# Reordering turns 3 to 14 of an attention backward kernel: K blocks, softmax, V quarters and stores in another order

## The chip, the cores and the metric

The kernel runs on one core of a Trainium2 chip. The metric is the device time of one execution in microseconds (us). Engines are named as in the profile: PE is TensorE, DVE is VectorE, ACT is ScalarE, POOL is GpSimd, SP is SyncE, which here issues almost all DMA transfers.

## The reference

One query per head attends to 8192 keys and values, for 32 heads of width 128, and the gradients of q, k and v are wanted as well as the output. All tensors are bfloat16.

```
B, H, Sq, Skv, Dh = 1, 32, 1, 8192, 128
def _fwd_reference(q, k, v):
    scale = q.shape[-1] ** -0.5
    scores = jnp.einsum('bhqd,bhkd->bhqk', q, k) * scale
    attn = _softmax(scores, axis=-1)
    return jnp.einsum('bhqk,bhkd->bhqd', attn, v)
...
_out, _vjp = jax.vjp(_f, q, k, v)
_grads = _vjp(grad_out)          # dq, dk, dv
```

With one query this is, per head: s = K q, p = softmax(s), out = pᵀV, dp = V·grad_out, ds = p (dp − Σ p dp) · scale, dq = dsᵀK, and the two large results dK = ds ⊗ q and dV = p ⊗ grad_out. K, V, dK and dV are 64 MiB each, 134 MB read and 134 MB written in all.

## The kernel before

**Tiling.** Two heads form one turn t; there are HP = 16 turns. In a turn K and V are tiles of 128 partitions x 128 rows x 128 columns, 4 MiB each. `k_in` has three such buffers, `v_in` two. dK and dV are written in place over K and V and stored from there, so a buffer's next load waits for its store.

**Steps of a turn** (NB = 8 blocks of 16 rows per partition):

- `k_block(t, c)`, lines 197 to 210: DVE transposes block c of K in 32x32 squares into an `XK` buffer (three buffers in pool `xkp`), and PE takes four matmuls from it into the scores bank `s`. A fourth transpose must wait until the first block's matmuls have left its buffer.
- `s_back`, `s_top`, `s_exp`, `s_sum`, `p_of`: the softmax. The scores come back by a DVE transpose, the maximum goes over PE and back to DVE (`nbias`), ACT takes the exponential, PE adds up (`s_sum`), DVE takes the reciprocal (`rinv`), ACT writes `p_rep` and the window `win_p`.
- dp = V·grad_out in two ways in the "wide" turns 3 to 14 (`wide(t)`): half of the rows by `v_part` = `v_bank` (PE transposes into one of three PSUM banks `psT`) + `v_copy` (ACT copies them out), followed by `v_scores` (PE); the other half by `v_block` (DVE transpose into an `XK` buffer) followed by `v_wide` (four PE matmuls). Both add into the bank `dp_ps`.
- `contract(t, "p")`: PE, 32 matmuls, out from V and `win_p`; `contract(t, "ds")`: PE, 32 matmuls, dq from K and `win_ds`.
- `outer(t, "p", r)` writes block r of dV, `outer(o, "ds", r)` writes block r of dK, both on DVE (line 366). The dK blocks of turn o = t − 1 are written in turn t by `dk(a, b)`, which stores dK after its last block.
- `v_back`, `pd_sum`, `ds_of`: dp comes back by a DVE transpose (line 315), Σ p dp goes over PE (line 324), `pdt` (line 329), ds on DVE, `win_ds` on ACT (line 244).
- `gather` takes out or dq of four turns out of the accumulator: out in turns 3, 7, 11 (behind `contract(t, "ds")`), dq in turns 4, 8, 12 (behind `pd_sum`). `prepare(t + 1)` spreads the next q and grad_out rows over the partitions.

**Order.** The instructions are put on each engine in the order of the program text (`manual_schedule`), and each engine works in that order. In a wide turn before the change DVE does: dK blocks 0 to 4; softmax with V blocks 0 and 1 between its steps and dK block 5; V blocks 2 and 3; dK blocks 6 and 7; dV blocks 0 and 1; `v_back`; dV block 2; `ds_of`; then dV blocks 3 to 7 alternating with K blocks 0 to 4 of the next turn; K blocks 5 to 7. SP issues per turn: store dK(t − 1), store dV(t), load K(t + 2), load V(t + 2).

Turns 1, 2 and 15 use another branch (all of V by `v_part`), turn 16 only finishes dK(15) and the small results.

Of the kernel before, what the change touches and what calls it, by code (L numbers as in the profile page):

```python
# [15 lines left out]
NB = 8  # L16
# [11 lines left out]
def kernel(  # L28
# [143 lines left out]
    dq_all = consts.tile([P, H], F32)  # L172

    def prepare(t):
        x = st[t] = {}
        x["m"] = psM.tile([P, 512], F32, tag="m", name="m_ps")
        for s in range(2):
            nc.tensor.matmul(x["m"][s * HF:(s + 1) * HF, 256:512],
                             lhsT=ident[0:H, 2 * t + s:2 * t + s + 1].to_broadcast([H, HF]),
                             rhs=rows[:].rearrange("h a d -> h (a d)"), start=True, stop=True, skip_group_check=True)  # L180
        x["qd"] = small.tile([P, 2, D], BF16, tag="qd", name="qd")
        nc.scalar.copy(x["qd"][:].rearrange("p a d -> p (a d)"), x["m"][:, 256:512])
# [12 lines left out]
            nc.scalar.copy(do_wide[a * QD:(a + 1) * QD, :, a * QD + SL - 1], do_four[a * QD:(a + 1) * QD, :, t])  # L195

    def k_block(t, c):
        x = st[t]
        X = xkpool.tile([P, BN, NW, QD], F32, tag="XK", name="XK_sb")
        nc.vector.transpose(X[:], Kt[t][:, c * BN:(c + 1) * BN, :].rearrange("p n d -> p (n d)").bitcast(F32).rearrange(  # L200
            "p (n w j) -> p n w j", n=BN, w=NW))
        if c == 0:
            x["s"] = psS.tile([P, 512], F32, tag="s", name="s_ps")
        cols = X[:].rearrange("p n w i -> p (n w i)").bitcast(BF16).rearrange(
            "p (n w i e) -> p w e n i", n=BN, w=NW, e=2)
        for w in range(NW):
            for e2 in range(2):
                nc.tensor.matmul(x["s"][:], lhsT=q_win[:, 2 * w + e2, SL - 1 - c:SL - 1 - c + P],  # L208
                                 rhs=cols[:, w, e2], start=(c == 0 and w == 0 and e2 == 0),
                                 stop=(c == NB - 1 and w == NW - 1 and e2 == 1), skip_group_check=True)  # L210
# [45 lines left out]
    def wide(t):  # L256
        return 3 <= t < HP - 1
# [22 lines left out]
    def v_scores(t, z):  # L280
        x = st[t]
        cols = x.pop(("XV", z)).rearrange("p m s -> p (m s)").bitcast(BF16).rearrange(
            "p (m s e) -> p e m s", s=P, e=2)
        if z == 0:
            x["dp"] = psD.tile([P, 512], F32, tag="dp", name="dp_ps")
        at = SL - 2 - 2 * z
        for e2 in range(2):
            for b in range(NQ):
                nc.tensor.matmul(x["dp"][b * QD:(b + 1) * QD, :], lhsT=do_win[:, b // 2, e2, at:at + QD],  # L289
                                 rhs=cols[:, e2, :, b * QD:(b + 1) * QD],  # L290
                                 start=(z == 0 and e2 == 0), stop=(not wide(t) and z == NZ - 1 and e2 == 1), skip_group_check=True)

    def v_block(t, r):

        X = xkpool.tile([P, NM, NW, QD], F32, tag="XK", name="XV_blk")
        nc.vector.transpose(X[:], Vt[t][:].rearrange("p n d -> p (n d)").bitcast(F32).rearrange(  # L296
            "p (m r w j) -> p m r w j", r=SL, w=NW, j=QD)[:, :, SL // 2 + r])
        st[t]["XW", r] = X

    def v_wide(t, r):  # L300
        cols = st[t].pop(("XW", r))[:].rearrange("p n w i -> p (n w i)").bitcast(BF16).rearrange(
            "p (n w i e) -> p w e n i", n=NM, w=NW, e=2)
        at = SL - 1 - (SL // 2 + r)
        for w in range(NW):
            for e2 in range(2):
                nc.tensor.matmul(st[t]["dp"][:], lhsT=do_wide[:, 2 * w + e2, at:at + P], rhs=cols[:, w, e2], start=False,  # L306
                                 stop=(r == SL // 2 - 1 and w == NW - 1 and e2 == 1), skip_group_check=True)

    def rows_in(x):
        return x.rearrange("p (m r) -> p m r", r=SL)  # L310
# [40 lines left out]
    def gather(t, which):  # L351
        S_ = backs.tile([P, 4, D], F32, tag="back", name="S_" + which)
        nc.scalar.copy(S_[:].rearrange("p j d -> p (j d)"), acc.pop(which)[:])
        bank, to = st[max(st)]["m"], (o_all if which == "p" else dq_all)
        pick = lane[:].rearrange("p (w j) -> p j w", j=4)
        at = 8 if which == "p" else 16
        for j in range(4):
            nc.tensor.matmul(bank[:, at:at + 2 * ST], lhsT=S_[:, j, :], rhs=pick[:, j, :],
                             start=(j == 0), stop=(j == 3), skip_group_check=True)
        nc.scalar.copy(to[:, 2 * (t - ST + 1):2 * (t + 1)], bank[:, at:at + 2 * ST])  # L360
# [104 lines left out]
    for t in range(1, HP + 1):  # L465
        o = t - 1
        now = t < HP
        parts = 4 if o == HP - 1 else 2 if o == HP - 2 else 1

        def dk(a, b):  # L470
            for r in range(a, b):
                outer(o, "ds", r)
                if (r + 1) % (NB // parts) == 0:
                    store(o, "ds", parts, r * parts // NB)

        blocks = now and wide(t)

        if blocks:

            dk(0, 5)  # L480
            s_back(t)
            s_top(t)
            for m in range(3):
                v_bank(t, m)
            v_block(t, 0)
            rs = s_exp(t)
            for m in range(3):
                v_copy(t, m)
            v_block(t, 1)
            v_part(t, 3)  # L490
            s_sum(t, rs)
            v_scores(t, 0)
            v_wide(t, 0)
            dk(5, 6)
            p_of(t)
            v_part(t, 4)
            v_part(t, 5)
            v_block(t, 2)
            v_wide(t, 1)
            v_part(t, 6)  # L500
            v_part(t, 7)
            v_block(t, 3)
            contract(t, "p")
            v_scores(t, 1)
            v_wide(t, 2)
            v_wide(t, 3)
            weights_do(t + 1)
            if wide(t + 1):
                weights_wide(t + 1)
        else:  # L510
            dk(0, 3)
            if now:
                v_part(t, 3)
                v_part(t, 4)
                s_back(t)
                s_top(t)
                v_scores(t, 0)
                v_part(t, 5)
                v_part(t, 6)
                rs = s_exp(t)  # L520
                for m in (7, 8, 9):
                    v_bank(t, m)
                s_sum(t, rs)
                v_copy(t, 7)
                v_copy(t, 8)
            dk(3, 4)
            if now:
                p_of(t)
                v_copy(t, 9)
                v_scores(t, 1)  # L530
                v_part(t, 10)
                v_part(t, 11)
                contract(t, "p")
                v_part(t, 12)
                v_part(t, 13)
                v_scores(t, 2)
                v_part(t, 14)
                v_part(t, 15)
                v_scores(t, 3)
                if t + 1 < HP:  # L540
                    weights_do(t + 1)
                    if wide(t + 1):
                        weights_wide(t + 1)
        if not now:
            dk(4, NB - 1)
            results()
            dk(NB - 1, NB)
            break
        dk(6 if blocks else 4, NB)
        fine = t == HP - 1  # L550
        outer(t, "p", 0)
        outer(t, "p", 1)
        if fine:
            store(t, "p", 4, 0)
        v_back(t)
        pd_sum(t)
        if t % ST == 0:
            gather(o, "ds")
        outer(t, "p", 2)
        ds_of(t)  # L560
        contract(t, "ds")
        if t % ST == ST - 1:
            gather(t, "p")
        if t + 1 < HP:
            prepare(t + 1)
        else:
            gather(t, "ds")
        for r in range(3, NB):
            outer(t, "p", r)
            if fine and r % 2:  # L570
                store(t, "p", 4, r // 2)
            if t + 1 < HP and t != 1 and r >= HALF - 1:
                k_block(t + 1, r - HALF + 1)
        if not fine:
            store(t, "p")
        if t == 1:
            for c in range(HALF + 1):
                k_block(t + 1, c)
        if t + 1 < HP:
            for c in range(HALF + 1, NB):  # L580
                k_block(t + 1, c)
                if not wide(t + 1):
                    v_part(t + 1, c - HALF - 1)
            if t + 2 < HP:
                weights_q(t + 2)
        if t + 2 < HP:
            load_k(t + 2)
            load_v(t + 2)
# [32 lines left out]
```

## Time and profile before

| quantity | before |
|---|---|
| median of 3 runs (lowest to highest) | 635.55 us (635.34 to 635.67) |
| the profiled execution's own time | 635.21 us |
| its span, first to last instruction | 633.4 us |
| granted PE clock, mean | 0.829 |
| DVE busy | 558.7 us (88%) |
| PE busy | 426.1 us (67%) |
| ACT busy | 156.9 us (25%) |
| bytes moved by DMA | 268.92 MB, mean 425 GB/s |

The span is 1.8 us shorter than the execution's own time, and that execution is 0.34 us below the median. Busy times are unions of an engine's instructions; a share of the whole span is an average over the start, sixteen turns and the end.

### The profile page before, as it was taken

The page shows a single profiled execution, that of the slowest core. Times are in us where ns is not written, and L with a number is a line of the kernel's source. Part 1 is how long each engine was busy: PE and PEld are TensorE (multiplying, and loading weights), DVE is VectorE, ACT ScalarE, POOL GpSimd, SP SyncE. Part 2 cuts the span into 40 slices and gives each one's busy share as a digit, 9 for nine tenths or more (in the row PEclk, how much of TensorE's full clock was granted, in tenths as well). Part 3 has the DMA queues.
Part 4 walks back from the last instruction along what each step waited for, and adds up shares of the span by engine and source line. Part 5 has one row for each costly group of instructions (what it writes and reads, how often), then busy time and mean ns, then how long its engine had stood idle before and what let it go on. Part 6 is the DMA issues. An engine that isn't in the chain of part 4 may idle for free.

```text
span 633.4 us, 7259 instructions
## 1 busy us (share of the span) xinstructions
PE 426.1 (67%) x2876; PEld 227.8 (36%) x2876; DVE 558.7 (88%) x662; ACT 156.9 (25%) x407; POOL 9.3 (1%) x27
## 2 busy tenths in 40 slices
PE   5968686478665767457776586756758667387950
PEld 2635252243423425134352342524415243152630
DVE  7688988989989899798998979899898998989891
ACT  1616052040311304114041220412304032040610
POOL 2000000000000000000000000000000000000000
PEclk9979597887788887878878888888898788987955
DMA  8999999999999999999999999999999999999996
GB/s 364 431 429 403 447 431 429 430 428 426 436 432 434 433 430 435 429 430 427 429 430 430 432 434 435 432 435 436 426 435 431 432 429 432 426 435 429 416 422 269
DMA packets 12177, 268.92 MB, mean 425 GB/s; under 512 B 1520, under 2 KB 1520, under 8 KB 1520
## 3 DMA queue, kind: packets, MB, share of 16 engines
q1 hardware_dynamic: 12048, 268.46, 98.9%
q8 instruction: 22, 0.36, 0.2%
q14 instruction: 11, 0.09, 0.0%
q10 hardware_dynamic: 96, 0.02, 0.0%
HBM read 134.23 MB, written 134.23 MB: 424 GB/s over the span
## 4 chain that ended last, share of the span: by engine, by line
DMA 42%; DVE 30%; PE 15%; issue 7%; ACT 3%; DVEq 0%; ACTq 0%; SPq 0%
DMA out_dram<-K 22%; DMA K<-in_k_dram 18%; DVE XK_sb L200 12%; DVE K L366 10%; PE T_ps L272 6%; DVE V L366 5%; PE dp_ps L306 3%; PE s_ps L208 2%; ACT XV_sb L278 2%; PE acc_p L344 2%; PE dp_ps L289 1%; DVE sT L215 1%; DMA rows<-in_grad_out_dram 1%; PE m_ps L223 1%; PE acc_ds L344 1%
## 5 line engine op out<-in xcount | busy, mean ns | idle before, releaser
L208 PE MATMUL s_ps<-XK_sb,q_win 128*128 128x512 bf16 x512 | 149.7, 433 | 50.0 <-DVE XK_sb L200 46.8
L200 DVE STREAM_TRANSPOSE XK_sb<-K 128x1024 f32<-128x1024 f32 x128 | 152.4, 1224 | 14.4 <-DMA K<-in_k_dram 12.0
L366 DVE TENSOR_TENSOR V<-p_rep,qd 128x2048 bf16<-128x2048 bf16 x128 | 151.9, 1205 | 2.9 <-ACT K L278 2.4
L366 DVE TENSOR_TENSOR K<-ds_rep,qd 128x2048 bf16<-128x2048 bf16 x128 | 147.8, 1209 | 0.1
L208 PEld LDWEIGHTS <-q_win 128*128 128x128 bf16 x512 | 53.7, 107 | 139.1 <-issue 103.7
L272 PE MATMUL T_ps<-ident_f,V 128*128 128x128 f32 x640 | 102.4, 320 | 0.1
L272 PEld LDWEIGHTS T_ps<-ident_f,V 128*128 128x128 f32 x640 | 91.7, 167 | 14.2 <-issue 2.2
L278 ACT COPY XV_sb<-T_ps 128x512 f32<-128x512 f32 x144 | 78.5, 587 | 69.5 <-PE T_ps L272 69.3
L344 PE MATMUL acc_ds<-K,win_ds 128*32 128x512 bf16 x512 | 50.7, 566 | 28.8 <-ACT win_ds L244 27.3
L296 DVE STREAM_TRANSPOSE XV_blk<-V 128x1024 f32<-128x1024 f32 x48 | 59.6, 1241 | 7.7 <-PE dp_ps L306 7.4
L223 PE MATMUL m_ps<-ident_f,top 128*128 128x128 f32 x16 | 6.5, 405 | 71.9 <-DVE top L222 71.9
L306 PE MATMUL dp_ps<-XV_blk,do_wide 128*128 128x512 bf16 x192 | 49.2, 387 | 0.0
L185 ACT COPY q_win<-q_blk 128x16 bf16<-128x16 bf16 x16 | 4.2, 261 | 159.8 <-PE s_ps L208 159.8
L344 PEld LDWEIGHTS <-win_ds 128*32 128x32 bf16 x512 | 16.3, 126 | 50.5 <-ACT win_ds L244 27.0
L344 PE MATMUL acc_p<-V,win_p 128*32 128x512 bf16 x512 | 30.9, 380 | 1.5 <-ACT win_p L244 1.5
L223 PEld LDWEIGHTS m_ps<-ident_f,top 128*128 128x128 f32 x16 | 2.6, 164 | 78.4 <-issue 73.2
L289 PE MATMUL dp_ps<-XV_sb,do_win 128*32 128x512 bf16 x288 | 24.1, 412 | 8.3 <-ACT XV_sb L278 8.1
L233 ACT ACTIVATE e<-sT,nbias 128x128 f32<-128x128 f32 x16 | 8.3, 520 | 80.7 <-DVE nbias L230 80.7
L306 PEld LDWEIGHTS <-do_wide 128*128 128x128 bf16 x192 | 16.9, 98 | 27.5 <-issue 13.0
L315 DVE STREAM_TRANSPOSE dpT<-dp_ps 128x512 f32<-128x512 f32 x16 | 11.5, 717 | 13.6 <-PE dp_ps L306 12.3
L324 PE MATMUL m_ps<-pd,same 128*128 128x1 f32 x32 | 6.3, 267 | 19.6 <-DVE m_ps L318 19.6
L344 PEld LDWEIGHTS <-win_p 128*32 128x32 bf16 x512 | 12.4, 96 | 14.4 <-issue 4.6
(68 smaller groups left out, 206.7 us busy)
## 6 DMA issues: line engine op xcount, KB each, us to landing
K<-in_k_dram SPq DMA_DIRECT2D x15, 4096.0 KB, 19.3
V<-in_v_dram SPq DMA_DIRECT2D x14, 4096.0 KB, 19.3
out_dram<-K SPq DMA_DIRECT2D x14, 4096.0 KB, 28.2
out_dram<-V SPq DMA_DIRECT2D x14, 4096.0 KB, 20.2
V<-in_v_dram SPq DMA_DIRECT2D x8, 1024.0 KB, 11.3
out_dram<-V SPq DMA_DIRECT2D x8, 1024.0 KB, 19.2
K<-in_k_dram SPq DMA_DIRECT2D x4, 1024.0 KB, 8.0
out_dram<-K SPq DMA_DIRECT2D x2, 2048.0 KB, 13.8
```

Of the source, the lines that this page charges most:

```text
L200: nc.vector.transpose(X[:], Kt[t][:, c * BN:(c + 1) * BN, :].rearrange("p n d -> p (n d)").bitcast(F32).rearrange("p (n w j) -> p n w j", ...
L208: nc.tensor.matmul(x["s"][:], lhsT=q_win[:, 2 * w + e2, SL - 1 - c:SL - 1 - c + P], rhs=cols[:, w, e2], start=(c == 0 and w == 0 and e2 == 0),
L223: nc.tensor.transpose(x["m"][:, 128:256], top[:].to_broadcast([P, P]), ident_f[:])
L233: nc.scalar.activation(e[:].rearrange("p (c n) -> p n c", c=NB), x["sT"][:, :, 0:NB], ACT.Exp, bias=nbias[:], scale=scale, accum_out=rs[:])
L272: nc.tensor.transpose(T_ps[:, j, :], words[:, at * P:(at + 1) * P], ident_f[:])
L278: nc.scalar.copy(x["XV", z][:, i * TB:(i + 1) * TB, :], x.pop(("T", m))[:])
L289: nc.tensor.matmul(x["dp"][b * QD:(b + 1) * QD, :], lhsT=do_win[:, b // 2, e2, at:at + QD], rhs=cols[:, e2, :, b * QD:(b + 1) * QD], start ...
L296: nc.vector.transpose(X[:], Vt[t][:].rearrange("p n d -> p (n d)").bitcast(F32).rearrange("p (m r w j) -> p m r w j", r=SL, w=NW, j=QD)[:, ...
L306: nc.tensor.matmul(st[t]["dp"][:], lhsT=do_wide[:, 2 * w + e2, at:at + P], rhs=cols[:, w, e2], start=False, stop=(r == SL // 2 - 1 and w = ...
L315: nc.vector.transpose(dpT[:].rearrange("p m r -> p (m r)"), x.pop("dp")[:])
L344: nc.tensor.matmul(acc[which][b * QD:(b + 1) * QD, :], lhsT=win[which][:, g, at:at + QD], rhs=X[:, 4 * g:4 * g + 4, :].rearrange("p n d -> ...
L366: nc.vector.tensor_tensor(X[:, a:b, :].rearrange("p n (a b) -> p n a b", b=R), x[which][:, a:b, :].unsqueeze(2).to_broadcast([P, BN, D // ...
```

## The change

Only the order in turns 3 to 14 changes; the compiled lists of instructions hold the same DVE, ACT, POOL and DMA work per turn, and the DMA transfers keep their order on SP. In a wide turn now:

- DVE: dK blocks 0 to 3; `s_back`, `s_top`; dK block 4; `nbias`; dK blocks 5 and 6; `rinv` and `p_of`; V blocks 0 to 3; dK block 7 with the store of dK; dV blocks 0 to 7 in four pairs; the store of dV; `v_back`, `pd_sum`, `ds_of`; all eight K blocks of the next turn in a row.
- PE: for each quarter i of V: `v_wide(i)`, a quarter of `contract(t, "p")` (8 matmuls), two `v_part`; after the fourth quarter both `v_scores`. The pair of dV blocks 2i and 2i + 1 overwrites the rows that quarter i has read.
- The accumulation in `dp_ps` is opened by `v_block`/`v_wide` and closed by `v_scores`, the other way round than before.

```
-        if z == 0:
+        if z == 0 and not wide(t):
             x["dp"] = psD.tile([P, 512], F32, tag="dp", name="dp_ps")
...
-            dk(0, 5)
+            dk(0, 4)
             s_back(t)
             s_top(t)
-            for m in range(3):
-                v_bank(t, m)
-            v_block(t, 0)
+            dk(4, 5)
             rs = s_exp(t)
-            for m in range(3):
-                v_copy(t, m)
-            v_block(t, 1)
-            v_part(t, 3)
             s_sum(t, rs)
-            v_scores(t, 0)
-            v_wide(t, 0)
-            dk(5, 6)
+            dk(5, NB - 1)
             p_of(t)
-            v_part(t, 4)
-            v_part(t, 5)
-            v_block(t, 2)
-            v_wide(t, 1)
-            v_part(t, 6)
-            v_part(t, 7)
-            v_block(t, 3)
-            contract(t, "p")
-            v_scores(t, 1)
-            v_wide(t, 2)
-            v_wide(t, 3)
+            for r in range(3):
+                v_block(t, r)
+            for i in range(4):
+                v_wide(t, i)
+                if i == 0:
+                    v_block(t, 3)
+                    dk(NB - 1, NB)
+                contract(t, "p", i * NG // 4, (i + 1) * NG // 4)
+                for z in range(2):
+                    v_part(t, z * (NM // TB) + i)
+                if i == 3:
+                    for z in range(2):
+                        v_scores(t, z)
+                outer(t, "p", 2 * i)
+                outer(t, "p", 2 * i + 1)
+            store(t, "p")
             weights_do(t + 1)
             if wide(t + 1):
                 weights_wide(t + 1)
+            early = NB
...
-        dk(6 if blocks else 4, NB)
...
-        for r in range(3, NB):
+        done = 0
+        for r in range(early + 1, NB):
             outer(t, "p", r)
...
-        if not fine:
+        if not fine and not blocks:
             store(t, "p")
-        if t == 1:
-            for c in range(HALF + 1):
+        if t + 1 < HP:
+            for c in range(done, NB):
                 k_block(t + 1, c)
...
```

## The prediction

> **What bounds the kernel now.** The page's slices come first, with the row of the DMA queue under them.
>
> ```profile
> DMA  8999999999999999999999999999999999999996
> GB/s 364 431 429 403 447 431 429 430 428 426 436 432 434 433 430 435 429 430 427 429 430 430 432 434 435 432 435 436 426 435 431 432 429 432 426 435 429 416 422 269
> ...
> q1 hardware_dynamic: 12048, 268.46, 98.9%
> ```
>
> From the second slice to the last but one the 16 DMA engines are full, at about 430 GB/s. At that rate the 268.5 MB take 624 us of the 633.4 us span, and the change moves the same bytes. So the page leaves almost nothing to gain, and the question is whether the new order starves the DMA. That is read from DVE, whose turns feed the stores. The windows view, one stretch per wide turn, each from the first dK block of a turn to that of the next (columns: length, PE, PE loads, DVE, ACT, POOL, clock, DMA share, GB/s; the last line sums turns 3 to 14):
>
> ```profile
> 274.61:313.32 38.71, 28.00 (x177) 15.18 (x175) 35.73 (x42) 9.22 (x25) 0.31 (x1) 0.78 1.01 433
> 313.32:352.04 38.72, 25.62 (x176) 13.80 (x175) 35.80 (x42) 9.22 (x25) 0.31 (x1) 0.87 1.00 432
> ...
> sum 469.19, PE 317.43 PEld 167.17 DVE 428.88 ACT 105.46 POOL 3.75; mean PE 26.45 PEld 13.93 DVE 35.74 ACT 8.79 POOL 0.31
> ```
>
> DVE is busy 428.88 of 469.19 us and idle 40.3 us, 3.4 us per turn. The waits of DVE in the same stretch say what for:
>
> ```profile
> DVE dpT L315 <- PE dp_ps L306: 12.3, 12, 1.4
> DVE XK_sb L200 <- DMA K<-in_k_dram: 10.6, 10, 2.5
> DVE XV_blk L296 <- PE dp_ps L306: 7.4, 12, 1.6
> DVE rinv L249 <- PE m_ps L238: 3.3, 9, 0.4
> DVE pdt L329 <- ACT dq_all L360: 2.0, 3, 0.8
> ```
>
> The second line is the DMA holding DVE back: K block 0 of the next turn waits for its load in 10 of 12 turns. Were DVE slower by those 10.6 us, it would merely wait less there.
>
> **How far DVE may fall behind.** At the end the stores must be issued before the queue runs dry. The view of DMA transfers gives issue to landing (KB, then median us):
>
> ```profile
> out_dram<-K SPq DMA_DIRECT2D x2, 2048.0 KB, 13.8
> out_dram<-K SPq DMA_DIRECT2D x4, 1024.0 KB, 11.7
> rows<-in_q_dram ACTq DMA_DIRECT2D x1, 8.0 KB, 3.3
> ```
>
> The first two are the last dK stores. Their own bytes take 4.9 and 2.4 us at 430 GB/s, and 3.3 us is what an 8 KB transfer needs on a queue with nothing ahead. What is left, 13.8 − 4.9 − 3.3 = 5.6 and 11.7 − 2.4 − 3.3 = 6.0, is time in which they stand behind other bytes. So I estimate a cover of 5.8 us: if turn 15 starts later than now by less than that, the end stays; beyond it each microsecond counts once.
>
> **Removed: 35.6 us of idle over turns 3 to 14.** All five waits above lose their cause. Dp's return had its last `v_wide` right ahead of it; now dV blocks 6 and 7 cover the last `v_scores`. V block 3 waited for a buffer while PE worked through `v_part`; now `v_wide` 0 (1.05 us) runs beside V blocks 1 and 2 (2.3 us). `rinv` gets dK blocks 5 and 6 as cover (2.26 us, by 5.72 us for five) for exponential 0.72 and sum 0.31 us. K block 0 starts about 11 us ahead of the turn's end instead of 13.6, so the load is there. The wait of `pdt` is counted anew below.
>
> **Added: `pdt` loses its cover.** dV block 2 stood between dp's return and `pdt`. Now DVE waits out `pd_sum` (0.38 us at L324) and the hops around it, about 0.5 us: 12 x 0.5 = 6.0 us. In turns 4, 8, 12 the gather of dq stands behind `pd_sum` on PE (1.06 us) with a copy on ACT (0.17), and today `pdt` waits for that copy: + 3 x 1.25 = 3.8 us (bounds 0, if it waits for `pd_sum` alone, and 3 x 2.0).
>
> **Added: K block 3 waits for K block 0.** The five dV blocks that stood between the K blocks are gone. From the end of ds, DVE needs 0.35 (`ds_rep`) + 3 x 1.135 (four K blocks in a row took 4.54 us now) = 3.8 us to reach the fourth transpose. PE, which must free its buffer, has `contract(t, "ds")` first, held until `win_ds` is written 0.69 us after ds. The timeline of PE in turns 5, 6 and 7:
>
> ```profile
> 219.27 3.60 PE L344 MATMUL acc_ds<-K,win_ds 128*32 128x512 bf16 x32 [1.79 <-ACT win_ds L244]
> 222.80 0.42 PE L178 MATMUL m_ps<-rows,ident 32*64 32x256 bf16 x2
> 223.16 2.82 PE L208 MATMUL s_ps<-XK_sb,q_win 128*128 128x512 bf16 x8
> ```
>
> ```profile
> 257.62 1.91 PE L344 MATMUL acc_ds<-K,win_ds 128*32 128x512 bf16 x32 [1.79 <-ACT win_ds L244]
> ```
>
> ```profile
> 298.02 3.60 PE L344 MATMUL acc_ds<-K,win_ds 128*32 128x512 bf16 x32 [1.79 <-ACT win_ds L244]
> 301.56 1.88 PE L358 MATMUL m_ps<-lane,S_p 128*128 128x8 f32 x8
> 303.69 0.42 PE L178 MATMUL m_ps<-rows,ident 32*64 32x256 bf16 x2 [0.25 <-ACT o_all L360]
> 304.04 2.31 PE L208 MATMUL s_ps<-XK_sb,q_win 128*128 128x512 bf16 x5
> ```
>
> The same 32 matmuls take 1.91 us at full clock and 3.60 at half; the mean over the twelve turns is 3.09 (37.1 us). One K block's four matmuls take 1.03 to 1.71 us, and I take 1.35. So block 0 leaves its buffer at 0.69 + 3.09 + 0.35 + 1.35 = 5.5 us and DVE waits 1.7 us, in nine turns 15.3 us. In turns 3, 7, 11 the gather of out lies between, and the K block starts 6.02 us after the contraction (298.02 to 304.04): 0.69 + 6.02 + 1.35 − 3.8 = 4.3 us, three times 12.8 us. After that PE (0.89 us per block at full clock) catches up with DVE's 1.135. Bounds: with contraction and block at full clock 0.2 us instead of 1.7; with both at half clock 0.69 + 3.60 + 0.35 + 1.71 − 3.8 = 2.6, and in turns 3, 7, 11 4.6.
>
> **Moved at no cost, and the cover.** The dV pairs wait for PE to have read their quarter. A quarter costs PE 0.89 (`v_wide`) + 0.48 (a quarter of 1.91) + about 0.95 (8 transposes) = 2.3 us against DVE's 2.26, and PE starts some 1.8 us ahead: V blocks 2 and 3 and dK block 7 hide it. Without that (first quarter at half clock) up to 0.45 us per turn, 5.4 us in all. The dK store comes 15.7 us into the turn instead of 16.7, the dV store some 13 us ahead of the turn's end instead of 4.4; both go behind bytes already queued. SP keeps its order (store dK, store dV, load K, load V): moved ahead, the store of dV waits for dV block 7 with nothing behind it but the two loads, which wait for the stores' landing anyway. On ACT `weights_do` and `weights_wide` (1.3 us) follow the last `v_scores` ahead of `win_ds`, which needs ds some 2 us later. POOL's clearing of `win_p` (0.31 us a turn) waits for the last quarter and is wanted a turn later.
>
> **Sum.** Added 6.0 + 3.8 + 15.3 + 12.8 = 37.9 us, removed 35.6: turn 15 starts 2.3 us later than now, within the cover of 5.8. The end stays with the DMA. On the profiled execution that is 635.2 us; I forecast **635.6 us**, the median of before (0.34 above that execution).
>
> **Rivals.**
>
> - *The half clock stays through the contraction and the first K block in every turn (slower).* Then 9 x 2.6 + 3 x 4.6 + 9.8 = 47.0 us are added; less 35.6 and the cover that is + 5.6 us: 641.2 us. With the dV pairs waiting too, + 11 us. It decides once the additions pass 41.4 us, 0.3 us per turn above my sum. For it: eleven of the twelve contractions now take more than 2.6 us instead of 1.91, and one K block more at half clock suffices. Against it: the dense K blocks give PE no pause, and turn 6 shows the same 3.4 us pause ahead of a contraction at full speed. The Trainium skill ("TensorE: Matmul & The Clock Gate", Part 1: The HAM clock gate) says that an idle window of about 3.4 us halves the clock, a busy one restores it, and the windows run free; by it a pause near 3.4 us may fall either way, as turns 5 and 6 do. Chance 0.37 for all slower cases.
> - *The drain gets shorter (faster).* From 626 to 634 us the DMA share is 0.23 in the windows view: 1.8 us of full work spread over 7.4 us, because engines finish unevenly. If the stores queued otherwise evened that out by half, some 2.5 us would go: 633.0 us. Nothing in the change addresses it. Chance 0.09.
> - *PE runs at full clock throughout.* Then DVE gets ahead and waits for K's loads as it does now: the forecast again, and part of its chance, 0.54.
>
> A comparison of this kernel can tell about 0.2% (1.3 us) from no change. Within that: 0.54; slower 0.37; faster 0.09. The range holds the forecast, half of the drain's gain and the slower cases up to + 7.5 us: 634.2 to 643.0.
>
> **What would show it.** Right: the GB/s row still near 430 to the last slices; DVE's waits at L315, L296 and L249 gone and the wait of K blocks for PE `s_ps` near 28 us in turns 3 to 14; the length of the twelve turns within 5.8 us of 469.2. Wrong: slices with a DMA digit below 9 ahead of the end, K blocks waiting over 35 us, or dV blocks waiting for PE at all.

## The result, and the profile after

| | before | after |
|---|---|---|
| median (lowest to highest) | 635.61 us (635.34 to 635.98, 4 runs) | 642.68 us (641.77 to 648.31, 4 runs) |
| the profiled execution | 635.21 us | 643.4 us |
| its span | 633.4 us | 641.6 us |
| granted PE clock, mean | 0.829 | 0.792 |

By the medians the kernel is 7.1 us slower. The ratio, 1.0129 with an interval of 1.0104 to 1.0154, is one of means and has the longest run in it: the four runs took 641.77, 641.96, 643.4 and 648.31 us, with a granted clock of 0.797, 0.795, 0.792 and 0.781. The forecast was no change. What came is nearest to the rival with the half clock, whose 641.2 us stand against a median of 642.68. Two executions of the experiments stand far outside and are left out of the ratios below: one of the kernel before (1196.14 us) and one of the kernel with more buffers (2029.97 us).

The page of the changed kernel, the slices of the DMA and its main queue:

```profile
DMA  8999999999999999999999999999999999999488
GB/s 364 441 432 390 447 428 424 437 435 433 426 433 434 434 424 429 436 437 428 426 427 444 430 427 428 439 431 430 425 438 435 420 413 426 424 425 427 198 369 370
...
q1 hardware_dynamic: 12048, 268.46, 97.9%
```

Up to the fourth slice from the end the rate is near 430 GB/s, as before. Then there is a hole in it: 198 GB/s. The stores are asked for too late, and the queue runs dry before the end. The windows view of the end shows the place (columns as in the prediction, the last two are DMA share and GB/s):

```profile
561.00:600.00 39.00, 25.93 (x175) 11.76 (x174) 36.55 (x43) 7.80 (x20) 0.31 (x1) 0.82 0.98 419
600.00:616.00 16.00, 13.13 (x131) 8.98 (x133) 13.86 (x18) 10.18 (x21) 0.31 (x1) 1.00 0.43 178
616.00:622.00 6.00, 3.00 (x42) 1.20 (x41) 5.44 (x11) 1.18 (x3) 0.00 (x0) 0.92 0.99 415
```

In the 16 us from 600 on, 0.57 of the engines' time is empty: 9.1 us. The DMA view says the same of the last dK stores, from issue to landing (13.8 us before):

```profile
out_dram<-K SPq DMA_DIRECT2D x2, 2048.0 KB, 7.1
```

The prediction counted 4.9 us for their own bytes and 3.3 us for an empty queue, 8.2 in all; at 7.1 us nothing stands ahead of them any more (and the two terms together were about 1 us too dear). The cover is used up.

How DVE fell behind is read from the windows of turns 3 to 14, here turns 7 and 8 as before, and the sum over the twelve:

```profile
276.21:320.19 43.98, 30.98 (x176) 14.71 (x175) 36.39 (x43) 9.45 (x25) 0.31 (x1) 0.69 1.01 434
320.19:361.73 41.54, 28.50 (x177) 13.65 (x175) 36.04 (x43) 9.45 (x25) 0.31 (x1) 0.75 1.00 432
...
sum 483.53, PE 327.11 PEld 152.01 DVE 431.78 ACT 108.23 POOL 3.73; mean PE 27.26 PEld 12.67 DVE 35.98 ACT 9.02 POOL 0.31
```

The twelve turns take 483.53 us where they took 469.19; turn 15 starts 14.15 us later (at 600.53 instead of 586.38). DVE works 2.9 us more and idles 11.4 us more (51.75 against 40.31). The waits of DVE in these turns (total us, times, longest):

```profile
DVE XK_sb L200 <- PE s_ps L208: 30.8, 15, 4.8
DVE pdt L332 <- ACT dq_all L363: 5.5, 3, 2.4
DVE pdt L332 <- PE m_ps L327: 5.1, 9, 0.7
DVE V L369 <- PE T_ps L272: 4.5, 7, 1.0
```

Every wait of the old list but that of `pdt` has gone. Now K blocks wait for PE 30.8 us, `pdt` 10.6 (2.0 before), the dV blocks 4.5 (6.0 with the short gaps that the view by groups counts). No K block waits for its load.

PE's timeline in turn 7 (start, length; in brackets the idle time ahead and who ended it) shows what clock PE had. Three stretches matter:

```profile
287.63 1.89 PE L309 MATMUL dp_ps<-XV_blk,do_wide 128*128 128x512 bf16 x4 [3.00 <-DVE XV_blk L297]
289.45 1.04 PE L347 MATMUL acc_p<-V,win_p 128*32 128x512 bf16 x8
290.43 1.97 PE L272 MATMUL T_ps<-ident_f,V 128*128 128x128 f32 x8
292.19 1.60 PE L309 MATMUL dp_ps<-XV_blk,do_wide 128*128 128x512 bf16 x4
...
295.20 1.04 PE L309 MATMUL dp_ps<-XV_blk,do_wide 128*128 128x512 bf16 x4
...
300.48 1.11 PE L289 MATMUL dp_ps<-XV_sb,do_win 128*32 128x512 bf16 x16 [0.24 <-ACT XV_sb L278]
303.49 0.53 PE L327 MATMUL m_ps<-pd,same 128*128 128x1 f32 x2 [1.91 <-DVE m_ps L321]
305.30 3.61 PE L347 MATMUL acc_ds<-K,win_ds 128*32 128x512 bf16 x32 [1.27 <-ACT win_ds L244]
308.84 1.88 PE L361 MATMUL m_ps<-lane,S_p 128*128 128x8 f32 x8
311.32 10.02 PE L208 MATMUL s_ps<-XK_sb,q_win 128*128 128x512 bf16 x32
```

From 277.37 to 287.63 PE has only 1.0 us of short matmuls, and the last pause is 3.00 us. Behind it the first quarter of V starts at half clock: `v_wide` takes 1.89 us and the transposes 1.97, where the third quarter has 1.04 and 1.09. The first quarter takes 4.56 us until the second begins, the third 2.44. In the kernel before, PE's long pause (5.85 us, up to 281.62) was followed by 16 transposes, and `v_wide` came only behind them:

```profile
281.86 3.62 PE L272 MATMUL T_ps<-ident_f,V 128*128 128x128 f32 x16
...
286.84 1.05 PE L306 MATMUL dp_ps<-XV_blk,do_wide 128*128 128x512 bf16 x4
```

There the transposes took the slow time (3.3 to 3.6 us where a merged row shows all 16 of them), and the first `v_wide` came at 1.05 us in eleven of twelve turns. In the new order it takes 1.89 us in all twelve. The transposes behind it take 1.91 to 1.97 us in seven turns and 1.09 to 1.76 in five, and the seven are those in which dV blocks wait: it is blocks 2 and 3, the second pair, that the delay reaches.

Behind the last scores PE has nothing but two short matmuls in 3.7 us (301.59 to 305.30), and the contraction takes 3.61 us instead of 1.91, the 32 K matmuls 10.02. DVE's timeline of the same place:

```profile
304.99 3.49 DVE L200 STREAM_TRANSPOSE XK_sb<-K 128x1024 f32<-128x1024 f32 x3
313.25 1.25 DVE L200 STREAM_TRANSPOSE XK_sb<-K 128x1024 f32<-128x1024 f32 x1 [4.77 <-PE s_ps L208]
314.95 1.25 DVE L200 STREAM_TRANSPOSE XK_sb<-K 128x1024 f32<-128x1024 f32 x1 [0.46 <-PE s_ps L208]
```

Three transposes, then a stop of 4.77 us at the fourth. That is the step "K block 3 waits for K block 0", in its dearest form.

### The profile page after: what moved, and what is told of

The parts are those of the page before. It is cut to its first block, busy times and chain, and to the rows that moved or that the text cites. A ratio compares the mean times of both kernels' runs of the same rounds, so it can differ in the third digit from the quotient of the medians.

```text
span 641.6 us, 7271 instructions
## 1 busy us (share of the span) xinstructions
PE 433.3 (68%) x2876; PEld 211.3 (33%) x2876; DVE 563.2 (88%) x662; ACT 159.1 (25%) x407; POOL 9.2 (1%) x27
## 4 chain that ended last, share of the span: by engine, by line
DVE 48%; PE 36%; issue 8%; DMA 4%; ACT 4%; DVEq 0%; ACTq 0%
DVE K L369 18%; DVE V L369 10%; DVE XK_sb L200 8%; PE T_ps L272 8%; PE acc_ds L347 7%; PE dp_ps L309 7%; PE s_ps L208 6%; PE acc_p L347 4%; DVE XV_blk L297 3%; DMA K<-in_k_dram 3%; DVE dpT L318 2%; DVE sT L215 2%; PE m_ps L361 1%; ACT win_ds L244 1%; PE m_ps L327 1%
## 5 line engine op out<-in xcount | busy, mean ns | idle before, releaser
L200 DVE STREAM_TRANSPOSE XK_sb<-K 128x1024 f32<-128x1024 f32 x128 | 149.1, 1215 | 34.5 <-PE s_ps L208 33.2
L208 PE MATMUL s_ps<-XK_sb,q_win 128*128 128x512 bf16 x512 | 134.8, 409 | 10.2 <-DVE XK_sb L200 6.2
L272 PE MATMUL T_ps<-ident_f,V 128*128 128x128 f32 x640 | 93.2, 294 | 0.1
L309 PE MATMUL dp_ps<-XV_blk,do_wide 128*128 128x512 bf16 x192 | 63.1, 459 | 36.1 <-DVE XV_blk L297 36.1
L272 PEld LDWEIGHTS T_ps<-ident_f,V 128*128 128x128 f32 x640 | 75.5, 150 | 34.1 <-issue 26.6
L208 PEld LDWEIGHTS <-q_win 128*128 128x128 bf16 x512 | 51.3, 103 | 86.8 <-issue 41.3
L297 DVE STREAM_TRANSPOSE XV_blk<-V 128x1024 f32<-128x1024 f32 x48 | 55.4, 1211 | 0.0
L347 PE MATMUL acc_p<-V,win_p 128*32 128x512 bf16 x512 | 42.7, 428 | 1.5 <-ACT win_p L244 1.5
L309 PEld LDWEIGHTS <-do_wide 128*128 128x128 bf16 x192 | 20.3, 111 | 55.2 <-DVE XV_blk L297 37.1
L289 PE MATMUL dp_ps<-XV_sb,do_win 128*32 128x512 bf16 x288 | 20.7, 383 | 5.2 <-ACT XV_sb L278 5.0
L238 PE MATMUL m_ps<-rs,same 128*128 128x1 f32 x32 | 8.3, 330 | 18.1 <-ACT e L233 18.1
L347 PEld LDWEIGHTS <-win_p 128*32 128x32 bf16 x512 | 9.2, 97 | 30.4 <-issue 28.5
## 6 DMA issues: line engine op xcount, KB each, us to landing
out_dram<-V SPq DMA_DIRECT2D x14, 4096.0 KB, 20.3
V<-in_v_dram SPq DMA_DIRECT2D x8, 1024.0 KB, 11.4
```

The costliest lines, as they stand in the source:

```text
L272: nc.tensor.transpose(T_ps[:, j, :], words[:, at * P:(at + 1) * P], ident_f[:])
L347: nc.tensor.matmul(acc[which][b * QD:(b + 1) * QD, :], lhsT=win[which][:, g, at:at + QD], rhs=X[:, 4 * g:4 * g + 4, :].rearrange("p n d -> ...
```

## The experiments

The theory after the result: DVE falls 14 us behind since PE works at half clock where the K blocks and the dV pairs wait for it; the end absorbs 5 to 6 us of that, and the rest is the loss. Rivals: three buffers for K blocks are too few at any clock; `pdt` is the term that tips it; or something at the end of the kernel changed, and the turns do not matter.

### How much may DVE fall behind? The kernel before, slowed

In the kernel before, dV block 2 of turn 14 is computed several times more. 12 more repeats:

```
         outer(t, "p", 2)
+        if t == HP - 2:
+            for _ in range(12):
+                outer(t, "p", 2)
```

> The kernel before, with dV block 2 of turn 14 computed twelve times more, at the same place (the same values again): 13.6 us of DVE work added shortly ahead of turn 15, nothing moved. It measures the cover at the end by itself. Theory (cover of about 6 us, beyond it one for one): 635.6 + 13.6 - 6 = 643 us, and the DMA runs dry only in the last slices. Rival (DVE's delay counts in full): 649 us. Rival (the DMA hides it): 635.6 us.

Measured: 643.61 us, ratio 1.013 (1.0115 to 1.0145). DVE's turn 15 starts 13.7 us late (600.08), the span is 8.8 us longer: 4.9 us absorbed, about as expected.

The same with 4 repeats:

> The kernel before, with dV block 2 of turn 14 computed four times more: 4.5 us of DVE work, the smaller sister of e8_delay12. Theory (cover of about 6 us): no change, 635.3 us. Rival (DVE's delay counts in full): 639.8 us.

Measured: 635.41 us, ratio 1.0003 (0.9993 to 1.0012). Turn 15 starts 3.4 us late (589.77), and the span is 0.1 us longer, as expected.

A delay made in one place gives the same end as the change: late by 13.7 us costs 8.8, late by 14.15 us costs 8.2. So the end needs no explanation of its own, and the loss is lateness less 5 to 6 us.

### The changed kernel once more, on another chip

> The changed kernel itself, on the chip of the other runs of this call, beside which they are to be read. 641.8 to 643.5 us, if it is as in its first runs; both theories say the same.

Measured: 648.2 us (642.14 to 649.56, 4 runs), ratio 1.0185 (1.0137 to 1.0232). The granted clock is 0.795 in the run of 642.14 us and 0.776 to 0.783 in the three others. The expected 641.8 to 643.5 us came in one run of four. In the profiled one (649.56 us) DVE idles 57.3 us in turns 3 to 14, of which K blocks 32.9, `pdt` 12.2 and dV blocks 7.9, and turn 15 starts 20.3 us late; the span is 14.4 us longer. 5.9 us are absorbed again. The first four runs show the same: the one of 648.31 us has the lowest clock. The time of one and the same program thus goes with the clock that PE was granted. That speaks for the theory, but does not show which is the cause: a PE that waits longer may also be granted less.

### PE kept busy in its pauses

Four matmuls of 128x512 behind the last `v_scores`, and four more between `pd_sum` and the dK contraction (`busy(n)` puts n matmuls of `ident` by `ident` into a `psT` bank, and nothing reads them). Nothing else is changed, and PE has more to do, not less:

```
                     for z in range(2):
                         v_scores(t, z)
+                    busy(4)
...
         if not blocks:
             outer(t, "p", early)
+        else:
+            busy(4)
```

> The changed kernel with added PE work whose result nobody reads: four matmuls 128x512 between the last v_scores and pd_sum, and four between pd_sum and the dK contraction, in turns 3 to 14, in the pause of about 4 us that PE makes there. Theory (half clock): PE's clock is halved by that pause; with the pause filled the contraction of dK takes 1.91 us instead of 3.6 in nearly all turns, the wait of K block 3 falls from 30.8 us in all to 5 to 12, and the time is 635.6 to 637 us although PE has more to do. Rival (PE is simply too busy, whatever its clock): the added matmuls only delay the contraction, the wait grows, and the time is 645 us or more.

Measured: 634.31 us (634.07 to 634.76), ratio 0.9983 (0.9974 to 0.9993), 1.3 us under the expected range. The waits of DVE in turns 3 to 14:

```profile
DVE XK_sb L200 <- DMA K<-in_k_dram: 6.7, 5, 3.3
DVE XK_sb L200 <- PE s_ps L208: 5.5, 5, 1.6
DVE V L369 <- PE T_ps L272: 4.7, 9, 0.7
DVE pdt L332 <- ACT dq_all L363: 4.7, 3, 1.6
DVE pdt L332 <- PE m_ps L327: 4.3, 9, 0.5
```

The wait of the K blocks falls from 30.8 to 5.5 us, and DVE waits for K's loads again: the DMA is what holds it. PE's timeline in turn 7 now has

```profile
297.98 1.02 PE L396 MATMUL D_ps<-ident 128*128 128x512 bf16 x4
299.39 1.91 PE L347 MATMUL acc_ds<-K,win_ds 128*32 128x512 bf16 x32 [0.39 <-ACT win_ds L244]
...
302.77 7.91 PE L208 MATMUL s_ps<-XK_sb,q_win 128*128 128x512 bf16 x32
```

The contraction is at 1.91 us in nine of the twelve turns (27.7 us in all, 41.3 in the changed kernel), the K matmuls at 7.91 instead of 10.02. In turn 7 the longest pause between the last scores and the contraction is 0.94 us. PE is given more work (435.3 us busy in all, 433.3 in the changed kernel) and DVE stops waiting for it, so the clock is shown as the cause of most of the K blocks' stall. The Trainium skill ("TensorE: Matmul & The Clock Gate", Part 1: The HAM clock gate) has the array throttled to half after an idle window of about 3.4 us. The runs agree for this pause: 3.7 us of near idleness give 3.61 us for the contraction, and filled it gives 1.91 in nine turns. They also show the halving behind shorter pauses, in the next kernel.

With the second four alone:

> The changed kernel with four extra 128x512 matmuls ahead of the dK contraction only (the four behind the last scores are left out). They write a spare part of PSUM that nobody reads. Theory: the pause right ahead of the contraction alone leaves PE at half clock for the contraction and the first K block, so filling it is enough: the waits of K blocks for s_ps in turns 3 to 14 fall from 29 to 31 us to under 12, and the time is 634 to 636. Rival: the clock is lost already in the earlier pause, between the last scores and the sums, and four matmuls are too short to restore it: the waits stay above 20 us and the time is 637 to 640.

Measured: 634.34 us, ratio 0.9983 (0.9973 to 0.9992).

```profile
DVE XK_sb L200 <- PE s_ps L208: 9.6, 7, 2.4
DVE XK_sb L200 <- DMA K<-in_k_dram: 5.8, 4, 1.9
```

Time and waits came as expected: four matmuls, 1 us of PE, ahead of the contraction are enough for the time. But the rival named in advance holds in four turns. In turns 5, 6, 9 and 13 the four matmuls themselves take 1.87 us instead of 1.02, so the clock was lost before them, behind 1.91 us of idling and the short sum, and the contraction takes 2.35 to 3.60 us. In turns 4, 8 and 12 they take 1.02 to 1.10 and the contraction still 3.18 to 3.40. In the other five, behind the same 1.91 us, both run at full speed. The contraction sums to 30.4 us, and the waits of 9.6 us fit into the cover.

### More buffers for K blocks

The two `XV` buffers, unused at that moment, take K blocks 0 to 3, so that seven blocks find room instead of three:

```
+        if wide(t) and c < 4:
+            if c % 2 == 0:
+                x["XB"] = xvpool.tile([P, NM, P], F32, tag="XV", name="XB_sb")
+            X = x["XB"][:, c % 2 * BN // 2:(c % 2 + 1) * BN // 2, :] ...
+        else:
+            X = xkpool.tile([P, BN, NW, QD], F32, tag="XK", name="XK_sb")[:]
...
```

> The changed kernel, but K blocks 0 to 3 of the wide turns are transposed into the two XV buffers, which are free at that time, so that seven K blocks have a buffer each instead of three. Nothing else moves. Theory (DVE lag): the changed kernel is late because DVE waits 30.8 us over turns 3 to 14 for PE to free a K block's buffer, so that turn 15 starts 14.2 us later and passes the cover of about 6 us. Without that wait turn 15 starts no later than before, DVE waits for K loads again, and the time is 635.6 us (within 1). Rival (queue): the earlier stores of dV disturb the DMA queue; then the time stays near 642 us though the buffer wait is gone.

Measured: 634.29 us, ratio 0.9986 (0.9976 to 0.9995), 0.3 us under the expected range. The rival of the disturbed queue is out: the stores of dV are as early here, and the loss is gone. The trace is of the execution of 2029.97 us (PE busy 1912.7 us of a span of 2028.2; the cause is not known), so the kernel was traced again:

> The kernel of e1_buffers once more (K blocks 0 to 3 in the free XV buffers), for a profile: its first profile came from a disturbed execution. Theory (DVE lag): 634.3 us as before; DVE's wait for PE to free a K block's buffer falls from 30.8 us to under 5, dK of turn 15's start lies at most 6 us behind that of the kernel before, and the DMA stays full to the end. Rival (the buffer wait only moves): 25 us or more of wait for PE turn up at the next step that needs the scores, the return of the scores at L215.

Measured: 634.32 us, ratio 0.9986 (0.9976 to 0.9995).

```profile
DVE XK_sb L206 <- PE s_ps L214: 18.8, 12, 5.7
DVE pdt L338 <- ACT dq_all L369: 4.7, 3, 1.6
DVE pdt L338 <- PE m_ps L333: 4.5, 9, 0.7
DVE V L375 <- PE T_ps L278: 2.2, 4, 0.9
```

The expected time came, but the expected wait did not: under 5 us was said, 18.8 remain, though turn 15 starts at 583.90, 2.5 us earlier than in the kernel before. With seven buffers it is K block 7 that waits, once per turn. So the lack of buffers is one of two conditions of the stall, and more buffers buy time rather than remove the cause: 12.0 us less at the K blocks, 1.4 at `pdt`, 2.3 at the V pairs. That is more than the 8.2 us beyond the cover, and the loss is gone.

### `pdt` covered again

dV block 7 and the store of dV go behind `pd_sum`:

```
-                outer(t, "p", 2 * i + 1)
-            store(t, "p")
+                if i < 3:
+                    outer(t, "p", 2 * i + 1)
...
+        if blocks:
+            outer(t, "p", NB - 1)
+            store(t, "p")
```

> The changed kernel with dV block 7 moved behind pd_sum, with the store of dV behind it: the cover that pdt had before. Theory (DVE lag): of the 10.6 us that pdt waits some 9 go, but dp's return now comes one dV block (1.13 us) sooner and waits about 0.4 us per turn for the last v_scores; net 4 to 5 us less lag, which counts one for one beyond the cover: 637 to 638.5 us. Rival (only the buffer wait matters, and PE sets when the contraction is done): no change, 642 us.

Measured: 634.68 us, ratio 0.9992 (0.9982 to 1.0001). 637 to 638.5 was expected: the gain is larger, a miss in size.

```profile
DVE XK_sb L200 <- PE s_ps L208: 26.8, 13, 3.6
DVE dpT L318 <- PE dp_ps L289: 3.9, 12, 0.3
DVE pdt L332 <- ACT dq_all L363: 3.1, 3, 1.0
DVE V L369 <- PE T_ps L272: 2.7, 5, 0.8
```

The K blocks still wait 26.8 us. `pdt` waits 3.1 instead of 10.6, K blocks and V pairs 4.0 and 1.8 less, `dpT` 3.9 more, and turn 15 starts at 589.45, 3.1 us later than in the kernel before: within the cover. At whichever of these waits DVE was relieved, some 8 us ended the loss. The expectation counted on less relief than came: why the K blocks and V pairs wait less too was not tested.

Both edits together:

> e1 and e2 together: K blocks 0 to 3 in the free XV buffers, and dV block 7 behind pd_sum. Theory (DVE lag): both take lag away, but e1 alone already ends under the cover, so nothing more can be won: 634.3 us, and DVE waits for K loads. Rival (the end depends on DVE's lead beyond the cover): another microsecond less, 633 us.

Measured: 634.51 us, ratio 0.9991 (0.9982 to 1.0000), K blocks wait 9.8 us for PE and 8.7 for loads. Nothing beyond either edit alone: under the cover, being earlier brings nothing.

### The V pairs

Matmuls also ahead of the transposes of the top rows (8) and behind the sums of the exponentials (6), on top of the kernel with two filled pauses:

> The changed kernel with the extra matmuls at both places of the contraction's pause, and further ones ahead of the transposes of the top rows (8) and behind the sums of the exponentials (6), so that PE enters the quarters of V with a shorter pause. Theory: the V pairs wait for the transposes because the first quarter runs at half clock; with these the first v_wide takes about 1.05 us instead of 1.89, the wait of V pairs for T_ps in turns 3 to 14 falls from 4.5 us to under 1.5, and the time stays at 634.3, since the DMA sets the end. Rival: the pairs wait since four matmuls, a quarter of the contraction and eight transposes are too long beside two DVE blocks even at full clock: the wait stays at 4 us or more. The extra matmuls on PE could also delay the exponential or the sums by up to 1 us a turn: then waits for m_ps at rinv would show it.

Measured: 636.16 us, ratio 1.0011 (1.0002 to 1.002). PE and DVE in turn 7, then the waits of DVE:

```profile
282.45 1.86 PE L309 MATMUL dp_ps<-XV_blk,do_wide 128*128 128x512 bf16 x4 [0.42 <-DVE XV_blk L297]
284.24 0.92 PE L347 MATMUL acc_p<-V,win_p 128*32 128x512 bf16 x8
285.09 1.09 PE L272 MATMUL T_ps<-ident_f,V 128*128 128x128 f32 x8
```

```profile
286.80 9.16 DVE L369 TENSOR_TENSOR V<-p_rep,qd 128x2048 bf16<-128x2048 bf16 x8
```

```profile
DVE XK_sb L200 <- DMA K<-in_k_dram: 17.0, 9, 2.9
DVE XK_sb L200 <- PE s_ps L208: 6.4, 5, 2.9
DVE pdt L332 <- ACT dq_all L363: 5.6, 3, 2.4
DVE pdt L332 <- PE m_ps L327: 4.3, 9, 0.5
```

The wait of the V pairs is gone from the list, and the eight dV blocks of a turn now run without a gap. The first `v_wide` was expected at about 1.05 us; it is there in five turns and at 1.58 to 1.86 in the other seven. But the transposes behind it take 1.09 us in all twelve, which is enough. DVE's work in the twelve turns is 428.30 us, where it was 431.78 with broken pairs and 428.88 before. The dV blocks are busy 109.9 us here and 112.4 in the changed kernel; with the K stall gone but the pairs still broken (the kernel with eight added matmuls per turn) DVE's work is 432.36. So the V pairs cost 6.0 us of idling and, by this comparison, some 2.5 of the 2.9 us of longer work. The cause is the half clock at the start of the V quarters: the wait goes with the slow transposes, in seven turns of the changed kernel and in none of this one. No run relieved the V pairs alone.

The time did not stay at 634.3 as expected: it is 1.8 us longer than with four matmuls per turn on the same chip (634.34), though DVE waits for loads 17.0 us, that is, has time to spare. What the additional matmuls (264 in all, 84 us of PE) slow in the transfers was not tested and stays open.

## Why the prediction was wrong, step by step

- **The DMA bounds the kernel, nothing is to be gained:** right. With DVE back in time, three edits take 634.3 us, 0.14 to 0.17% less than the kernel before, though DVE enters turn 15 up to 4.8 us earlier. That small gain is clear of the noise (upper ends of the intervals 0.9992 to 0.9995); it is below what was called measurable, and its place was not isolated.
- **Removed, 35.6 us:** right in size. The new idle time is 30.8 + 10.6 + 6.0 = 47.4 us, the whole rose by 11.4, so 36.0 went. For the 10.6 us of waiting for K's loads the reason given (the K blocks start later) is not shown: where DVE is not late, 6.7 and 5.8 us of it are back.
- **`pdt`, 9.8 us:** measured 10.6 (5.1 for nine turns, 5.5 for the three with the gather). Right.
- **K block 3 waits for K block 0, 28.1 us:** measured 30.8, the mechanism as described. The nine ordinary turns cost 1.55 to 2.30 us each, 16.4 for 15.3; the three with the gather of out 3.9, 5.7 and 4.8, 14.4 for 12.8. The size was off by 2.7. The term took the contraction at 3.09 us, the mean of before; the new order has it at 3.44 (41.3 / 12), and at 3.36 or more in eleven of the twelve turns. That is 0.35 us a turn too little, of which 0.2 reached the wait.
- **V pairs, at no cost:** this is the step that failed. It priced a quarter of V at 2.3 us, from rows at full clock of the old order, where 16 transposes stood between PE's pause and the first `v_wide`. In the new order nothing stands there: the first quarter began at half clock in all twelve turns (4.56 us in turn 7), and the pairs cost 6.0 us idle and some 2.5 us of work. The bound of 5.4 us for just this case was nearly the idle time, and it was left out of the sum.
- **The cover, 5.8 us:** right to about 1 us. 14.15 − 8.2 = 5.9 here, 5.9 on the other chip, 4.9 in the delayed kernel.
- **The sum:** lateness 2.3 us forecast, 14.15 found. The difference is V pairs 6.0, longer work 2.9 (mostly theirs), K blocks 2.7, `pdt` 0.8, less 0.4 more removed and 0.2 for turn 3's start. With the V pairs at nothing, the rest would have come to some 5.6 us, at the edge of the cover. The slower rival's total, 47.0 added, is close to the 47.4 that came, but its split is not: it had K blocks at 37.2 and the pairs at nothing, where 30.8 and 6.0 were measured. Its addition for waiting dV pairs, + 11 us in all, is above the 7.1 that came. The 2.9 us of longer work were in neither.
- **The signs named:** the waits at L315, L296 and L249 gone (yes), K blocks near 28 us (30.8, and not the 35 named as wrong), twelve turns within 5.8 us of 469.2 (no, + 14.3). Two signs of being wrong came: a DMA digit of 4 ahead of the end, and dV blocks that wait for PE at all.
- **The weighing:** "turn 6 shows the same 3.4 us pause ahead of a contraction at full speed" was the argument against the rival. One turn in twelve was little ground. The prediction had seen the other eleven at 2.6 us or more; behind such a pause the slow end should have been taken, and a forecast 3.5 us from its own tipping point, resting on a mean, should not have been the likeliest case.

## What to carry to other kernels

Price a PE step at half clock wherever the new order leaves PE idle ahead of it for about 3 us (here 3.0 us ahead of the V quarters, slow in twelve turns of twelve, and 3.7 ahead of the contraction, slow in all twelve too, at 2.46 us or more), and add up all such places before comparing with the slack, as each alone may look harmless. A price read in the old order holds only if what stands ahead of the step stays the same. Where PE paces another engine through a small ring of buffers, a pause of PE that costs the other engine nothing in itself can slow the next work that it waits for (the K blocks waited 1.6 to 5.7 us per turn here); 1 us per turn of matmuls without use, ahead of the critical ones, was worth 8 us in all here. In a kernel bound by its transfers, find the slack first by delaying one engine by a known amount: the kernel before took 3.4 us without loss, and of 13.7 us it lost all but 4.9.

## What the runs showed of the hardware that was not expected

- The granted clock does not only vary between runs, it repeats. In the changed kernel on the other chip turns 7 to 10 and turns 11 to 14 take the same time to 0.1 us (44.0, 41.5, 40.2 and 38.1 us, at a clock of 0.69, 0.75, 0.75 and 0.82 both times). The execution of 643.4 us differs from that by over 0.2 us only in turns 3, 4, 11 and 12. It may be that the turns and the changes of the clock fall into step; that was not tested.
- The contraction that comes behind the gather of dq stayed at 3.2 to 3.5 us in turns 4, 8 and 12 in both kernels with the pause ahead of it filled. Why was not tested.
- The kernel with 264 additional matmuls ends 2.0 us later than the one with eight per turn (spans of 634.3 and 632.3 us), with the same bytes. DVE enters turn 15 only 1.0 us later (582.83 against 581.85), still 3.5 us ahead of the kernel before.
